# Pooled attention and mixture of depths on one core: leftover products of two token chunks together, other chunks, counts that read PSUM, another order

## The chip, the cores and the metric

One core of a Trainium2 chip runs the whole program. The metric is the device time of one execution in microseconds (us), lower is better. The engines: TensorE (PE in the profile, its weight loads PEld), VectorE (DVE), ScalarE (ACT), GpSimd (POOL), SyncE (SP, which here only issues DMAs).

## The reference, cut to what matters

```python
# q, k, v: (8 batches, 8 heads, 576 tokens, 64) float32
k_p = k.reshape(B, H, 72, 8, D).mean(axis=3)          # 8 tokens pooled to 1: 72 keys
v_p = v.reshape(B, H, 72, 8, D).mean(axis=3)
attn = softmax(q @ k_p.T / sqrt(D))
x = heads side by side of (attn @ v_p)                 # (8, 576, 512)
scores = einsum('bsd,d->bs', x, w_gate); out = x.copy()
for b in range(B):
    top = the 128 tokens of the largest scores[b]
    ye = relu(x[b, top] @ w1) @ w2                     # w1 512x1024, w2 1024x512
    out[b, top] = x[b, top] + sigmoid(scores[b, top])[:, None] * ye
```

Everything is float32. A batch is 3.5 MB of q, k and v; w1 and w2 are 4 MB.

## The kernel before

Each batch passes two parts. The **front** (one per batch, 0 to 7) is attention, the store of x and the choice of 128 tokens. The **dense** part (also one per batch) is the two matrix products on those tokens and the scatter of their rows.

*Front.* SP issues the loads of k, q and v. There is one k buffer (`kr`) and there are two each of q and v, so the load of k of the next batch waits until k is pooled. k and v of batch 0 are pooled on PE, the others on DVE or POOL (L530, L531; L618 to L624). DVE transposes pooled k (L539) and q (L558, in two halves of 16 and 20 of the 36 steps). The scores are made with the keys on the partitions. 72 keys don't fit two heads on 128 partitions, so the last 64 keys of each head are products of 32x64 tiles (L576), and the 8 *leftover keys* of four heads together are products of 128x32 tiles (L585). ACT takes the exponentials (L590 into `em`, L594 into `el`). The 576 tokens are then taken in five *chunks* (four of 128 tokens, number 4 of 64). For each chunk PE multiplies with the pooled v: 16 main products in 64x64 tiles (L663), then 4 leftover products in 64x64 tiles (L667), into one pair of PSUM banks. The columns beside v give the softmax sum and the token's score; ACT or DVE takes them (L681 to L685), DVE inverts (L689), ACT or DVE normalises into `xs` (L698, L700), and SP or ACT stores `xs` to `out` (L396).

*Rank.* When all chunks of a batch have their sums, DVE makes the scores (L716, L717), PE spreads them over all partitions (L737, a transpose of a broadcast), ACT or DVE copies that row from PSUM into `sr` (L408, L410), and for each chunk one DVE instruction counts how many scores are larger (L749, five per batch). From the ranks come a one-hot matrix (L756 to L760), on PE the list of the chosen tokens (L766), the indices (`tk`, L770; `ix`, L774 on POOL), and POOL issues an indirect DMA (L775) that gathers the 128 rows from `out` into `xr`, for which all five stores of the batch must have landed.

*Dense.* PE transposes `xr` (L796), multiplies with w1 (L805, 64 products of 128 columns per batch), ACT or DVE applies relu, PE multiplies with w2 (L819, 8 products of 512 columns), DVE makes `y` (L824), POOL scatters (L828).

*Fillers.* Eight steps named `busy` (L847) multiply the identity by itself, four products each, while PE would have nothing to do.

*Order.* A class `Plan` collects some 777 steps with engines, priorities and dependencies. What is built is fixed by three tables of numbers in the source: `ORDER` (the order of all steps), `HOMES` (the PSUM banks of each PSUM job) and `TURNS` (which of its possible engines a step takes). Each engine runs its steps in the order of the table; waits follow from the data. PSUM has 8 banks: the scores of a half take banks 0 to 3, a chunk takes one pair of four, a `ONES` job one bank.

Of the kernel before, what the change touches and what calls it, by code (L numbers as in the profile page):

```python
# [96 lines left out]
"""  # L97
TABLE = [[int(x) for x in t.split()] for t in (ORDER, HOMES, TURNS)]
ON_PE = (0,)
AGO = 500  # L100


class Plan:


    SWITCH = 0.2

    def __init__(self):
# [1147 lines left out]
```

## Time and profile before

| | |
|---|---|
| runs (us) | 249.0, 250.75, 251.26; median 250.75 |
| the profiled execution | 249.6 us; its profile spans 247.8 us |
| PE busy | 220.0 us, 89% |
| DVE, POOL, ACT busy | 146.1, 106.9, 83.4 us |
| moved by DMA | 46.82 MB |
| mean granted TensorE clock | 0.965 |

Times in the profile count from the start of the span. A busy PE is modelled from the matmuls' sizes, so how long a group of products really takes is read from the starts of the groups behind it. One float32 matmul of the program shows as two records (x32 is 16 products).

### The profile page before, as it was taken

The numbers are of one execution on the slowest core, as the hardware profiler recorded it, in microseconds if no ns is written. First come the engines' busy times: TensorE is split into PE (matmuls) and PEld (weight loads), VectorE is DVE, ScalarE is ACT, GpSimd is POOL, SyncE is SP. The second block draws the span as 40 slices with busy tenths as digits, with TensorE's granted clock in tenths as the row PEclk, the third lists the DMA queues.
The fourth block names the chain that finished last, engine by engine and source line by source line (L and its number), as shares of the span: only waits on it lengthen the run. The fifth ranks groups of instructions, "written<-read, shape, count | busy, mean of one in ns | idle before, by whom it ended". The sixth has DMA issues, their size and how long they took to land.

```text
span 247.8 us, 7329 instructions
## 1 busy us (share of the span) xinstructions
PE 220.0 (89%) x3074; PEld 155.9 (63%) x3074; DVE 146.1 (59%) x357; ACT 83.4 (34%) x282; POOL 106.9 (43%) x147
## 2 busy tenths in 40 slices
PE   2799869497959999999989999999999999999980
PEld 2497537255648935795438789674588869656740
DVE  2589985997991683896587699448094603200210
ACT  2004564675635352257236644335011000201000
POOL 7023782992695639797760534020071302210310
PEclk9999999779968999999999999999999999999996
DMA  6998999997799959839750122414312101110101
GB/s 195 363 329 307 379 354 323 393 355 277 266 314 380 335 225 346 329 128 352 296 187 4 50 103 87 127 49 129 125 46 83 28 20 42 42 42 3 52 33 56
DMA packets 16329, 46.82 MB, mean 189 GB/s; under 512 B 1696, under 2 KB 1696, under 8 KB 14496
## 3 DMA queue, kind: packets, MB, share of 16 engines
q1 hardware_dynamic: 12016, 37.23, 41.7%
q10 hardware_dynamic: 2992, 4.85, 6.1%
q0 software_dynamic: 1280, 4.20, 5.0%
q8 instruction: 26, 0.43, 0.7%
q14 instruction: 15, 0.12, 0.1%
HBM read 34.73 MB, written 11.53 MB: 187 GB/s over the span
## 4 chain that ended last, share of the span: by engine, by line
PE 60%; DMA 16%; POOL 11%; issue 5%; DVE 4%; SPq 1%; POOLq 0%; DVEq 0%; ACT 0%
PE pJ L819 10%; PE pG L805 9%; DMA xr<-out_dram,ix 8%; DMA vr<-in_v_dram 8%; PE pA L805 7%; PE pJ L805 7%; PE pG L819 6%; PE pG L663 3%; PE pA L819 3%; POOL vr L618 3%; PE pG L667 2%; PE pG L576 2%; POOL vr L623 2%; POOL vs L624 1%; POOL vr L628 1%
## 5 line engine op out<-in xcount | busy, mean ns | idle before, releaser
L819 PE MATMUL pJ<-w,ht 128*128 128x512 f32 x80 | 37.7, 602 | 0.0
L749 DVE SCALAR_TENSOR_TENSOR cmp<-sr,sc,lat 128x576 bf16<-128x576 f32 (+1 forms) x40 | 35.3, 883 | 0.9
L774 POOL TENSOR_SCALAR ix<-tk 128x1 int32<-128x1 f32 x8 | 2.9, 368 | 54.2 <-DVE gv L783 19.3
L558 DVE STREAM_TRANSPOSE qt<-qr 128x1280 f32<-128x1280 f32 (+1 forms) x16 | 21.7, 1362 | 5.7 <-DMA qr<-in_q_dram 5.7
L618 POOL TENSOR_TENSOR vr<-vr 128x512 f32<-128x512 f32 (+1 forms) x12 | 18.6, 1563 | 11.8 <-DMA vr<-in_v_dram 11.8
L805 PEld LDWEIGHTS pG<-xg,w 128*128 128x128 f32 x192 | 22.4, 192 | 1.8 <-issue 1.8
L805 PE MATMUL pG<-xg,w 128*128 128x128 f32 x192 | 23.1, 276 | 0.0
L819 PEld LDWEIGHTS pJ<-w,ht 128*128 128x128 f32 x80 | 14.0, 190 | 14.0 <-issue 13.6
L828 POOL DMA_INDIRECT out_dram<-y,ix x8 | 8.9, 1109 | 30.4 <-DVE y L824 15.0
L590 ACT ACTIVATE em<-pG 128x1280 f32<-128x1280 f32 (+1 forms) x16 | 18.1, 1129 | 11.5 <-PE pG L585 11.1
L576 PE MATMUL pG<-qt,kt 32*64 32x320 f32 (+1 forms) x512 | 20.8, 429 | 1.3 <-ACT em L590 1.3
L805 PEld LDWEIGHTS pJ<-xg,w 128*128 128x128 f32 x160 | 18.6, 192 | 1.8 <-issue 1.4
L805 PEld LDWEIGHTS pA<-xg,w 128*128 128x128 f32 x160 | 18.5, 192 | 1.8 <-issue 1.8
L805 PE MATMUL pJ<-xg,w 128*128 128x128 f32 x160 | 19.4, 277 | 0.0
L805 PE MATMUL pA<-xg,w 128*128 128x128 f32 x160 | 19.0, 276 | 0.0
L576 PEld LDWEIGHTS pG<-qt,kt 32*64 32x64 f32 x512 | 10.1, 136 | 9.1 <-issue 2.8
L819 PE MATMUL pG<-w,ht 128*128 128x512 f32 x32 | 14.4, 592 | 0.0
L824 DVE SCALAR_TENSOR_TENSOR y<-pG,gv,xr 128x512 f32<-128x512 f32 x2 | 1.5, 752 | 21.3 <-PE pG L819 21.3
L689 DVE RECIPROCAL rz<-za 128x8 f32<-128x8 f32 (+1 forms) x40 | 7.2, 189 | 11.1 <-ACT za L681 8.7
L663 PEld LDWEIGHTS pG<-vs,em 64*64 64x64 f32 x448 | 11.6, 146 | 3.5 <-issue 2.0
L698 ACT ACTIVATE xs<-pG,rz 128x64 f32<-128x64 f32 (+1 forms) x56 | 12.1, 348 | 4.0 <-DMA out_dram<-xs 3.4
L663 PEld LDWEIGHTS pA<-vs,em 64*64 64x64 f32 x416 | 9.8, 140 | 5.0 <-ACT ss L682 1.9
(171 smaller groups left out, 406.5 us busy)
## 6 DMA issues: line engine op xcount, KB each, us to landing
vr<-in_v_dram SPq DMA_DIRECT2D x8, 1024.0 KB
kr<-in_k_dram SPq DMA_DIRECT2D x7, 1152.0 KB
qr<-in_q_dram SPq DMA_DIRECT2D x7, 1152.0 KB
out_dram<-xs ACTq DMA_DIRECT2D x17, 256.0 KB
w<-in_moe_w_dram SPq DMA_DIRECT2D x4, 1024.0 KB
out_dram<-xs SPq DMA_DIRECT2D x15, 256.0 KB
vr<-in_v_dram SPq DMA_DIRECT2D x16, 64.0 KB
out_dram<-xs SPq DMA_DIRECT2D x6, 128.0 KB
```

The costliest lines, as they stand in the source:

```text
L558: nc.vector.transpose(out=QT[b % 2][h].rearrange("p j t c -> p t j c"), in_=QR[b % 2][:, lo:hi].rearrange("p t (j e) -> p t j e", j=2))
L576: note(nc.tensor.matmul(pG[64 * s : 64 * s + 64, r, 0:n], KT[i][rows, j, (SP - NL) * s + NL : (SP - NL) * s + SP], tokens(j, s, rows, 0, h ...
L590: note(nc.scalar.activation(EM[h][i], pG[:, :, 0:n], AF.Exp, scale=exp_scale))
L618: engine(e).tensor_tensor(out=x[:, a:z, 0:4], in0=x[:, a:z, 0:4], in1=x[:, a:z, 4:8], op=OP.add)
L623: engine(e).tensor_tensor(out=x[:, :, 0:2], in0=x[:, :, 0:2], in1=x[:, :, 2:4], op=OP.add)
L663: note(nc.tensor.matmul(acc[64 * z : 64 * z + 64, s, E * m : E * m + E], EM[h][i][64 * s : 64 * s + 64, m, m0 + 64 * z : m0 + 64 * z + 64] ...
L689: nc.vector.reciprocal(RZ[i][rows, c], ZA[rows, b, c])
L698: note(nc.scalar.activation(to[:, s, m], o[:, s, m, 0:D], AF.Copy, scale=rz[:, NP * s + m : NP * s + m + 1]))
L749: nc.vector.scalar_tensor_tensor(cmp[0:n], SR[0:n], SC[i][0:n, c : c + 1], LAT[0:n, LAST - OFF[c] : LAST - OFF[c] + S], op0=OP.subtract, o ...
L805: note(nc.tensor.matmul(single(ju)[:, cap * f : cap * f + cap], w1[g][:, d, 128 * f : 128 * f + 128], XG[i][:, d, :], start=(d == 0), stop ...
L819: note(nc.tensor.matmul(single(jd)[0:cap, :], HT[i][f // 4][:, f % 4, :], w2[f // 4][:, f % 4, :], start=(f == 0), stop=(f == FB - 1)))
L828: j = nc.gpsimd.indirect_dma_start(out=out_rows, out_offset=bass.IndirectOffsetOnAxis(ap=IX[x][:, :1], axis=0), in_=Y[i], in_offset=None)
```

## The change

1. **Chunks.** A chunk was 8 of the 36 steps by all 16 groups of tokens; chunks 0 to 3 are now 16 steps by 8 groups, chunk 4 is 4 steps by 16 groups. In a store, the outermost dimension is now 16 (before 8, for chunk 4 it was 4). `q` is transposed into a layout with runs of 8, and the exponentials of the second half and of the leftover keys take three ACT instructions each (`spread`) so that each chunk is contiguous in `em` and `el`.
2. **Leftover keys.** Their scores for all tokens of a batch are one step of 8 products of 320 columns in a PSUM bank of its own (before 8 of 128 and 8 of 192 columns beside the main scores). The leftover products with v now run in 32x64 tiles for two chunks together: chunks 0 with 2, 1 with 3, and 4 alone; both chunks' PSUM pairs are held until then.
3. **Rank.** The copies into `sr` are gone: the spread row stands in a pair of banks and the five counts of DVE read it there. The two sums of `tk` and `gv` are one reduction.
4. **Loads.** The gate vector is loaded in rows of 1792 bytes in place of 256.
5. **Order.** All three tables are new: 753 steps.

The diff, cut to its core (the tables left out but for one line):

```diff
-    2 4 10 21 3 12 14 31 9 19 16 8 6 13 91 18 17 22 5 36 20 15 23 11 7 37 24 25 26 38 39 40 41 770 32 33 42 34 35
+    2 4 9 19 3 5 12 10 21 11 741 16 6 14 20 0 746 17 34 29 13 18 85 22 23 24 25 8 89 26 88 87 30 7 31 35 36 15 37 38
...
-    TN = (8, 8, 8, 8, 4)
+    TN = (16, 16, 16, 16, 4)
+    GN = (8, 8, 8, 8, 16)
+    ALONG = ((0, 2), (1, 3), (4,))
...
-            nc.vector.transpose(out=QT[b % 2][h].rearrange("p j t c -> p t j c"),
-                                in_=QR[b % 2][:, lo:hi].rearrange("p t (j e) -> p t j e", j=2))
+            nc.vector.transpose(out=QT[b % 2].rearrange("p j x t g -> p t (j x) g")[:, lo:hi],
+                                in_=QR[b % 2][:, lo:hi].rearrange("p t (x g) -> p t x g", g=8))
...
-            for s in range(2):
-                for z in range(halves):
-                    note(nc.tensor.matmul(acc[64 * z : 64 * z + 64, s, 0 : NP * E], EL[h][i][64 * s : 64 * s + 64, l0 + 64 * z : l0 + 64 * z + 64],
-                                     VL[i][64 * s : 64 * s + 64, u].rearrange("p m e -> p (m e)"),
-                                     start=False, stop=True, skip_group_check=True))
+                for s in range(2):
+                    for z in range(2):
+                        for c in cs:
+                            if z < ROWS[c] // 64:
+                                x = 64 * s + 32 * SIDE[c]
+                                note(nc.tensor.matmul(pair(jobs[c])[64 * z : 64 * z + 64, s, 0 : NP * E], EL[i][x : x + 32, AT[c] + 64 * z : AT[c] + 64 * z + 64],
+                                                      VL[i][x : x + 32].rearrange("p m e -> p (m e)"),
+                                                      start=False, stop=True, skip_group_check=True), jobs[c])
...
-                copy(e, SR[:, OFF[a] : OFF[a] + w], single(j_)[:, 0:w])
...
-                nc.vector.scalar_tensor_tensor(cmp[0:n], SR[0:n], SC[i][0:n, c : c + 1], LAT[0:n, LAST - OFF[c] : LAST - OFF[c] + S],
-                                               op0=OP.subtract, op1=OP.is_gt, accum_out=RK[0:n, b, c])
+                note(nc.vector.scalar_tensor_tensor(cmp[0:n], row()[0:n, 0:S], SC[i][0:n, c : c + 1], LAT[0:n, LAST - OFF[c] : LAST - OFF[c] + S],
+                                                    op0=OP.subtract, op1=OP.is_gt, accum_out=RK[0:n, b, c]))
```

DVE, from the scores of batch 0 (`sc0`) to its token list (`tk0`), before, from the first count on (L749 counts, L689 and L700 end chunks, L558 transposes q of batch 3, L716 and L717 already make the scores of batch 1):

```order
L749 SCALAR_TENSOR_TENSOR cmp_119,rk_115<-sr_114,sc0_109,lat_116 128x576
L558 STREAM_TRANSPOSE qt11_81<-qr1_69 128x20x2x32
L749 SCALAR_TENSOR_TENSOR cmp_119,rk_115<-sr_114,sc0_109,lat_116 128x576
L689 RECIPROCAL rz1_108<-za_148 128x8
L749 SCALAR_TENSOR_TENSOR cmp_119,rk_115<-sr_114,sc0_109,lat_116 128x576
L632 TENSOR_REDUCE vs0_90<-vr0_70 128x5
L642 COPY vs0_90<-vs0_90 32x66 x2
L646 TENSOR_TENSOR vl0_92<-vs0_90,inside_160 128x528
L749 SCALAR_TENSOR_TENSOR cmp_119,rk_115<-sr_114,sc0_109,lat_116 128x576
L689 RECIPROCAL rz1_108<-za_148 128x8
L700 TENSOR_TENSOR xs10_100<-pA_169,rz1_108 128x2x4x64
L749 SCALAR_TENSOR_TENSOR cmp_119,rk_115<-sr_114,sc0_109,lat_116 64x576
```

and now (L777 makes `sc0`, L589 transposes q of batch 2, L570 pooled k of batch 2):

```order
L777 TENSOR_REDUCE sc0_105<-ss0_101 128x5
L589 STREAM_TRANSPOSE qt0_78<-qr0_68 128x20x8x8
L805 SCALAR_TENSOR_TENSOR cmp_114,rk_110<-pA_162,sc0_105,lat_111 128x576 x3
L570 STREAM_TRANSPOSE kh_73<-ks_72 128x9x64
L805 SCALAR_TENSOR_TENSOR cmp_114,rk_110<-pA_162,sc0_105,lat_111 128x576
L805 SCALAR_TENSOR_TENSOR cmp_114,rk_110<-pA_162,sc0_105,lat_111 64x576
L746 RECIPROCAL rz1_104<-za_143 128x8 x2
```

Between `sc0` and the first count there stood eleven other instructions before, now one. From the last count to `tk0` follow, now: the ends of four chunks of batch 1, `qt0` of batch 2 (first half), `kh` and `qt1` (first half) of batch 3.

PE, before the first transposed gather, of batch 0 (`xr0`), before (L576 and L585 are the scores of batch 3, L663 and L667 chunks of batch 2):

```order
L585 MATMUL pG_168<-qt11_81,kl1_77 32x192 x8
L663 MATMUL pA_169<-vs0_90,em10_84 64x66 x8
L667 MATMUL pA_169<-vl0_92,el10_88 64x264 x2
L663 MATMUL pJ_170<-vs0_90,em00_82 64x66 x16
L667 MATMUL pJ_170<-vl0_92,el00_86 64x264 x4
L576 MATMUL pG_168<-qt10_80,kt1_75 64x256 x16
L585 MATMUL pG_168<-qt10_80,kl1_77 32x128 x8
L796 MATMUL pA_169<-ident_151,xr0_132 128x128 x4
L663 MATMUL pJ_170<-vs1_91,em11_85 64x66 x16
```

and now (L611 and L628 are the scores of batch 3, L798 spreads the scores of batch 1, L702 and L714 are chunks of batch 2):

```order
L611 MATMUL pG_161<-qt1_79,kt1_75 64x256 x16
L798 MATMUL pJ_163<-ident_146,sc1_106 128x128 x4
L798 MATMUL pJ_163<-ident_146,sc1_106 128x64
L611 MATMUL pG_161<-qt1_79,kt1_75 64x320 x16
L628 MATMUL pA_162<-qt1_79,kl1_77 32x320 x8
L849 MATMUL pA_162<-ident_146,xr0_127 128x128 x4
L702 MATMUL pG_161<-vs0_86,em00_80 64x66 x16
L702 MATMUL pG_161<-vs0_86,em10_82 64x66 x16
L714 MATMUL pG_161<-vl0_88,el0_84 64x264 x8
L702 MATMUL pJ_163<-vs0_86,em10_82 64x66 x8
L714 MATMUL pJ_163<-vl0_88,el0_84 64x264 x2
```

The transposed gather (L796, now L849) stood behind all five chunks of batch 2 and stands now ahead of them; all eight fillers now stand ahead of it, before seven (the eighth was at the end). On POOL the first gather stood behind the pooled v of batches 2 and 3, and stands now behind that of batch 2 alone. On SP, the first half of w1 came after k, q and v of batches 0 to 3, and comes now after k and q of batch 4 as well.

## Rows read from the trace of the kernel before

**Rows 1.** The page, part 1: busy time, share of span and instructions.

```profile
PE 220.0 (89%) x3074; PEld 155.9 (63%) x3074; DVE 146.1 (59%) x357; ACT 83.4 (34%) x282; POOL 106.9 (43%) x147
```

**Rows 2.** Windows: stretch and length in us, busy us by engine, clock, DMA share, GB/s.

```profile
0.00:60.00 60.00, 45.11 (x869) 31.52 (x869) 45.75 (x84) 24.73 (x92) 33.33 (x57) 0.94 0.92 327
0.00:70.97 70.97, 53.14 (x1044) 36.97 (x1044) 55.21 (x105) 31.59 (x111) 39.92 (x64) 0.94 0.91 323
46.00:53.00 7.00, 6.29 (x128) 3.84 (x128) 6.91 (x14) 5.37 (x24) 6.76 (x7) 0.51 1.04 379
70.00:77.00 7.00, 6.03 (x124) 4.62 (x124) 4.48 (x12) 0.58 (x1) 4.28 (x6) 0.52 1.02 353
70.97:239.70 168.73, 165.90 (x2023) 118.20 (x2024) 89.83 (x249) 51.81 (x171) 65.96 (x83) 0.98 0.40 140
```

**Rows 3.** Timeline of PE, 0 to 75 us: start, length, what, idle before.

```profile
46.71 1.16 PE L663 MATMUL pJ<-vs,em 64*64 64x66 f32 x32 [3.68 <-ACT xs L698]
...
70.97 1.09 PE L796 MATMUL pA<-ident,xr 128*128 128x128 f32 x4 [2.94 <-DMA xr<-out_dram,ix]
```

**Rows 4.** Timeline of DVE, 10 to 75 us: the rank of batch 0.

```profile
33.48 0.20 DVE L717 TENSOR_REDUCE sc<-ss 128x5 f32<-128x40 f32 x1 [0.26 <-DVE ss L716]
...
63.67 0.12 DVE L770 TENSOR_REDUCE tk<-pA 128x1 f32<-128x2 f32 x1
```

**Rows 5.** The chain of waits in order of time: start, length, what.

```profile
63.88 0.82 POOL ix L774
...
64.99 5.84 DMA xr<-out_dram,ix
...
85.84 7.53 DMA xr<-out_dram,ix
...
130.09 1.05 PE pG L576 x32
131.14 0.57 PE pG L585 x16
...
154.81 1.26 PE pG L576 x32
156.07 0.79 PE pG L585 x16
...
239.71 0.76 DVE y L824
```

**Rows 6.** Timeline of PE in two chunks, 138 to 140 us.

```profile
138.41 0.70 PE L663 MATMUL pJ<-vs,em 64*64 64x66 f32 x32
138.93 0.62 PE L667 MATMUL pJ<-vl,el 64*64 64x264 f32 x8
139.37 0.65 PE L663 MATMUL pG<-vs,em 64*64 64x66 f32 x32
139.84 0.72 PE L667 MATMUL pG<-vl,el 64*64 64x264 f32 x8
```

**Rows 7.** Groups by line and shape: busy us, mean ns of one, idle before.

```profile
L749 DVE SCALAR_TENSOR_TENSOR cmp<-sr,sc,lat 128x576 bf16<-128x576 f32 x32 | 28.9, 902 | 0.6
L558 DVE STREAM_TRANSPOSE qt<-qr 128x1280 f32<-128x1280 f32 x8 | 12.0, 1501 | 5.7 <-DMA qr<-in_q_dram 5.7
L558 DVE STREAM_TRANSPOSE qt<-qr 128x1024 f32<-128x1024 f32 x8 | 9.8, 1222 | 0.0
L539 DVE STREAM_TRANSPOSE kh<-ks 128x576 f32<-128x576 f32 x8 | 9.7, 1214 | 0.1
L689 DVE RECIPROCAL rz<-za 128x8 f32<-128x8 f32 x32 | 6.0, 192 | 5.9 <-ACT za L681 4.6 <-ACT ht L812 1.2
L749 DVE DVE_READ_ACCUMULATOR cmp<-sr,sc,lat 128x1 f32 x32 | 2.6, 81 | 0.0
L700 DVE TENSOR_TENSOR xs<-pA,rz 128x512 f32<-128x512 f32 x7 | 4.8, 692 | 0.4
L847 PE MATMUL pG<-ident 128*128 128x128 f32 x40 | 5.4, 283 | 0.0
```

More of the change, by code (lines that the diff above doesn't have):

```diff
@@ L147, in listed @@
         for o in ops:
-            if o["job"] is not None:
-                jobleft[o["job"]] += 1
+            for j in (o["job"], o["job2"]):
+                if j is not None:
+                    jobleft[j] += 1
         ready = [0.0] * len(ops)
@@ L159, in listed @@
         order = []
+        mates = {}
+        for o in ops:
+            if o["job2"] is not None:
+                mates[o["job"]], mates[o["job2"]] = o["job2"], o["job"]
+        first = {}
+        for n, o in enumerate(ops):
+            if o["job"] is not None:
+                first.setdefault(o["job"], n)
+        due = []
         def homes(j):
@@ L163, in homes @@
                 return None
+            if due and j not in due:
+                return 1e9, None
+            if j in mates and not due:
+                if left[first[mates[j]]] or sum(all(held[x] is None for x in h) for h in self.jobs[j]) < 2:
+                    return 1e9, None
             best = None
@@ L213, in listed @@
             order.append(n)
-            j = o["job"]
-            if j is not None:
+            for j in (o["job"], o["job2"]):
+                if j is None:
+                    continue
                 jobend[j] = max(jobend[j], done)
@@ L368, in direct_path, with note @@
     beside = {}
-    def note(ins):
+    def note(ins, other=None):
         n, e, j, needs = plan.now
+        if other is not None:
+            j = other
         if j is None:
@@ L642, in again @@
                     nc.vector.tensor_copy(to, of)
-        both((("DVE", 0.35), ("ACT", 0.42)), False, again, [("VS", i)], [("VS2", i)], p, name=f"vd{b}")
+        both((("DVE", 0.42), ("ACT", 0.5)), False, again, [("VS", i)], [("VS2", i)], p, name=f"vd{b}")
         def spread(e):
             engine(e).tensor_tensor(
-                out=VL[i].rearrange("p u m e -> p (u m) e"),
-                in0=VS[i][:, NP : NP + 1, :].to_broadcast([128, 2 * NP, E]),
-                in1=inside.rearrange("p u (m one) -> p (u m) one", one=1).to_broadcast([128, 2 * NP, E]), op=OP.mult)
@@ new lines, in spread, with attend, main, go @@
+                out=VL[i], in0=VS[i][:, NP : NP + 1, :].to_broadcast([128, NP, E]),
+                in1=inside.rearrange("p (m one) -> p m one", one=1).to_broadcast([128, NP, E]), op=OP.mult)
+        both((("DVE", 0.4), ("POOL", 0.62)), False, spread, [("VS", i), ("VS2", i), "VS1", "inside"], [("VL", i)], p, name=f"vl{b}")
+    def attend(b):
+        i = b % 2
+        jobs = [plan.job(PAIRS) for c in range(NC)]
+        def main(c):
+            h, j_ = int(SIDE[c]), jobs[c]
+            def go():
+                acc = pair(j_)
+                for m in range(NP):
+                    for s in range(2):
+                        for z in range(ROWS[c] // 64):
+                            note(nc.tensor.matmul(acc[64 * z : 64 * z + 64, s, E * m : E * m + E],
+                                                  EM[h][i][64 * s : 64 * s + 64, m, AT[c] + 64 * z : AT[c] + 64 * z + 64],
+                                                  VS[i][64 * s : 64 * s + 64, m, :], start=(m == 0), stop=False, skip_group_check=True))
+            add("PE", 0.52, go, [("EM", h, i), ("VS", i), ("VS2", i), "VS1"], [], 100 * b + 5 + c, mode=6464, job=j_, name=f"a{b}{c}")
+        def more(cs):
+            def go():
+                for s in range(2):
+                    for z in range(2):
[5 more added lines that the diff above has]
+                                                      start=False, stop=True, skip_group_check=True), jobs[c])
+            add("PE", 0.5, go, [("EL", i), ("VL", i)], [], 100 * b + 5 + cs[-1], mode=3264, job=jobs[cs[0]],
+                job2=jobs[cs[1]] if len(cs) > 1 else None, name=f"al{b}{cs[0]}")
+        for cs in ALONG:
+            for c in cs:
+                main(c)
+            more(cs)
+        for c in range(NC):
+            after(b, c, jobs[c])
@@ L672, in attend, with after @@
+    def after(b, c, j_):
+        n, i = ROWS[c], b % 2
         rows = slice(0, n)
@@ L707, in kept @@
             store.setdefault(b, []).append(x)
-        dma(out[b].rearrange("(g t) d -> t g d", g=G)[T0[c] : T0[c] + TN[c]], XS[i][c][rows], n * 2048, 100 * b + 4,
-            [("XS", i, c)], [("ROWS", b, c)], then=kept, rate=260e3, cost=0.62, free=True, name=f"o{b}{c}")
+        to = out[b].rearrange("(g t) d -> t g d", g=G)[T0[c] : T0[c] + TN[c], G0[c] : G0[c] + GN[c]]
+        if c == NC - 1:
+            to = to.rearrange("t g d -> g t d")
+        dma(to, XS[i][c][rows], n * 2048, 100 * b + 4,
+            [("XS", i, c)], [("ROWS", b, c)], then=kept, rate=360e3, cost=0.68, free=True, name=f"o{b}{c}")
     def rank(b):
@@ L717, in score @@
             nc.vector.tensor_reduce(out=SC[i], in_=SS[i], axis=AX.X, op=OP.add)
-        add("DVE", 0.76, score, [("RZ", i, c) for c in range(NC)], [("SC", i)] + [("SS", i, c) for c in range(NC)], p - 70,
+        add("DVE", 0.52, score, [("RZ", i, c) for c in range(NC)], [("SC", i)] + [("SS", i, c) for c in range(NC)], p - 70,
             name=f"sc{b}")
@@ L722, in pieces, with row, spread @@
             a, g = AUX[i], engine(e)
-            g.tensor_copy(a[:, :, 2], SC[i])
-            g.tensor_tensor(out=R1, in0=SC[i], in1=a[:, :, 2], op=OP.subtract)
-            g.tensor_copy(a[:, :, 3], R1)
-            g.tensor_tensor(out=R1, in0=R1, in1=a[:, :, 3], op=OP.subtract)
+            g.tensor_copy(a[:, :, 3], SC[i])
+            g.tensor_tensor(out=R1, in0=SC[i], in1=a[:, :, 3], op=OP.subtract)
             g.tensor_copy(a[:, :, 4], R1)
+            g.tensor_tensor(out=R1, in0=R1, in1=a[:, :, 4], op=OP.subtract)
+            g.tensor_copy(a[:, :, 5], R1)
         both((("DVE", 0.9), ("POOL", 1.45)), False, pieces, [("SC", i), "AUX0"], [("AUX", i), "R1"], p - 65, name=f"pc{b}")
-        for half, (a, z) in enumerate(((0, 3), (3, NC))):
-            w = sum(ROWS[a:z])
-            j_ = plan.job(ONES)
-            def spread(a=a, z=z, j_=j_):
-                for c in range(a, z):
-                    o = OFF[c] - OFF[a]
-                    note(nc.tensor.transpose(single(j_)[:, o : o + 128], SC[i][:, c : c + 1].to_broadcast([128, 128]), ident))
-            add("PE", 0.115 * (z - a) + 0.05, spread, [("SC", i), "ident"], [], p - 70, job=j_, name=f"sp{b}{half}")
-            def keep(e, a=a, w=w, j_=j_):
-                copy(e, SR[:, OFF[a] : OFF[a] + w], single(j_)[:, 0:w])
-            both((("DVE", 0.12 + 1.05e-3 * w), ("ACT", 0.15 + 0.87e-3 * w)), False, keep, [], [("SR", half)], p - 70, job=j_,
-                 name=f"ke{b}{half}")
+        jr = plan.job(PAIRS)
+        def row():
+            return pair(jr).rearrange("p a b -> p (a b)")
+        def spread():
+            for c in range(NC):
+                n = ROWS[c]
+                note(nc.tensor.transpose(row()[:, OFF[c] : OFF[c] + n], SC[i][0:n, c : c + 1].to_broadcast([n, 128]), ident[0:n, 0:n]))
+        add("PE", 0.72, spread, [("SC", i), "ident"], [], p - 70, job=jr, name=f"sp{b}")
         for c in range(NC):
@@ L760, in one_hot @@
                     nc.vector.tensor_scalar(OH[:, c, :], slots, RK[:, b, c], None, op0=OP.is_equal)
-        both((("DVE", 1.45), ("ACT", 2.1)), True, one_hot, [("RK", b, c) for c in range(NC)] + ["slots", "ones"], ["OH"], p + 0.6, name=f"oh{b}")
+        both((("DVE", 1.35), ("ACT", 2.45)), True, one_hot, [("RK", b, c) for c in range(NC)] + ["slots", "ones"], ["OH"], p + 0.6, name=f"oh{b}")
         j_ = plan.job(ONES)
```

179 lines of the change are left out of this document (90 added, 89 removed), and 85 rows, old and new, of tables (HOMES, ORDER, TURNS).

## The prediction

> **What bounds the kernel now.** I read the page first: PE is busy 220.0 of 247.8 us, DVE 146.1 [rows 1], so the kernel ends when PE has done its work, and only two things matter: how much work that is, and where PE stands idle or runs at a lower clock. The windows cut the span at 70.97 us, where PE transposes the first gathered rows and dense work begins [rows 2, 3]. Behind that point PE is busy 165.90 of 168.73 us, 2.8 us idle. Ahead of it PE is busy 53.14 of 70.97, 17.8 us idle, while DMA moves 327 GB/s over the first 60 us. In two stretches of 7 us, at 46 and at 70 us, the granted clock is 0.51 and 0.52, half of it at 1.2 GHz in place of 2.4 [rows 2]; PE had idled 3.68 and 2.94 us just before [rows 3]. At half speed the 6.29 and 6.03 busy us are 3.1 and 3.0 us of work, so the second part of each is lost.
>
> In full-speed time PE does 53.14 - 3.1 = 50.0 us of work ahead of 70.97 and 165.90 - 3.0 = 162.9 behind it, 212.9 together. From the end of its last product (239.71) to the end of the span are 8.1 us, and 1.8 us more to the execution's own 249.6.
>
> Why 70.97? The chain of waits and the timeline of DVE tell: the scores of batch 0 exist at 33.68 [rows 4], but its token list only at 63.67. Then the path is fixed: index, indirect DMA, PE starts 7.3 us after the list's start [rows 3 to 5]. Thirty us of rank for five counts of 0.90 + 0.08 us [rows 7] is order and not work: other instructions of DVE stand between.
>
> **The change, part by part.**
>
> *First gather (order, counts from PSUM).* This is the largest term. In the new order one transpose stands between the scores and the counts, and behind them four chunk ends, two transposes of q and two of k before the list. I sum DVE from the durations [rows 7]: one q transpose 1.50; five counts of 0.98, 4.9; two k transposes 2.4; four inversions and normalisations of 0.19 + 0.69, 3.5; one pair of small copies from PSUM, which I set at 0.3; two q transposes 2.4. That is 15.1 us. Ahead of the scores the same attention of batch 0 must be done, so I keep 33.68: the list at 48.8. The other path to it is data: the transpose of q of batch 3 stands right before the list. Up to that q SP and ACT issue (sizes from the tensors' shapes) four batches of k and q, 9.4 MB, v 4.7, gate 0.2, five stores 1.2: 15.5 MB, at 327 GB/s [rows 2] 47.4 us, plus 1.22 for the transpose 48.6. Both paths agree. With 7.3 us the first transposed gather starts at 56.2; the second gather of the trace took 7.53 against 5.84 [rows 5], which would be 57.9. I take **57**, 14 us earlier. What is late next: the first half of w1, now behind k and q of batch 4. Up to it 19.5 MB, 59.6 us; PE has batch 2's five chunks to do there (4.3 us), so it hides.
>
> *Work done by then.* Of the 50.0 us, five chunks of batch 2 are no longer ahead: a chunk is 0.47 + 0.44 [rows 6], 4.6 us. One more filler is, 1.1 (40 records, 8 to a filler, are 5.4 us [rows 7]).
>
> *Scores of leftover keys.* Products of 192 columns took 0.79, of 128 0.57 [rows 5], so 64 columns are 0.22 and the fixed part is 0.13. One step of 320 in place of two saves 0.13, over 8 batches 1.1 us. The main scores keep columns and shape.
>
> *Leftover products.* Within the 64x64 tiles a chunk's leftover takes 0.44 [rows 6]. Two chunks together on 32-row tiles take the same 264 columns once, if their eight products run beside each other as those of L576 do: 64 columns there cost 0.21, the time of two rounds of 64, for 16 products [rows 5]. Five times 0.44 becomes three times: -0.88 per batch. Against it stands the change of tile shape, three times in and out. Rows 5 give a fixed part of 1.05 - 4 x 0.21 = 0.21 for L576 and 0.57 - 2 x 0.22 = 0.13 for L585; a chunk's main products right behind another shape take 0.52 against 0.47 [rows 6]. I take 0.15 in and 0.05 out, three times 0.20: net -0.3, over 8 batches **-2.4 us**. The bounds: no cost at all, -7.0; 0.21 both ways, +3.0. The Trainium skill speaks against this part: "TensorEngine Tiling (Array Packing)", Key Properties, says that changing the tiling mode drains TensorE. The fixed parts of rows 5 agree with it; without the rule the sum would end 4.6 us lower.
>
> *Transposes of q.* Their output now lies in runs of 8 elements. The trace has runs of 32 (1.17 ns per element) and, for k, single elements nine apart (2.1 ns) [rows 7]. Runs of 8 are nearer the first; I take no cost. The other end is 0.9 ns x 2304 = 2.1 us of DVE per batch.
>
> *Three exponentials for one, twice per batch:* ACT is busy 34% [rows 1] and has room for some 0.5 us per batch; without that cover it delays the banks of the scores by as much. *Copies into `sr` gone, fewer reductions:* some 1 us per batch less for DVE and ACT, inside the idle time of both once PE is the bound. *Stores, gate:* they change how the same bytes move; hidden behind PE after 57 us, and before it only 1.2 MB are stores. *PSUM:* the spread row now holds a pair of banks until the last count; zero if PE has other steps with free banks, see the rivals.
>
> **The sum.** Work ahead of the gather: 50.0 - 4.6 + 1.1 - 0.5 (four score steps) - 0.6 (two batches' chunks) = 45.4. Work in all: 212.9 + 1.1 - 1.1 - 2.4 = 210.5. Behind the gather: 165.1. From 57 that is 222.1; idle time behind it as before 2.8 plus 1 for the tighter first steps; one stretch at half clock half the time, as PE will still idle some us ahead of 57: 1.5. End of PE 227.4, plus 8.1 and 1.8: 237.3 against the profiled 249.6, which lies 1.15 under the median of the runs. So **238** us on the scale of the runs.
>
> **Rivals.**
>
> 1. *Only half of the early gain* (0.20). DVE doesn't run through its queue: it is busy 55.21 of the first 70.97 us [rows 2] and every instruction ahead of the list can wait for POOL or PE. Dear transposes alone (seven halves ahead of the list, 7 us) would do it. Gather at 64: 245.
> 2. *The gather is early and nothing follows* (0.12). The windows show DMA at 327 GB/s from the start; if w1 or k of batch 4 lands 10 us after my 59.6, since k has one buffer and POOL must empty it, PE waits there what it waited before. Left is the work saved, some 2 to 3 us: 248.
> 3. *The other side: PSUM held by the counts* (0.09). Before, a copy freed the bank after about half a us; now two of eight banks stay taken for at least 4.9 us of counts, longer where transposes stand between, and in the order the chunk that takes the pair next (of batch 1) stands directly behind. If PE waits for it in each of the 8 ranks, the gain of 12.7 is gone at 1.6 us per rank; at 2 us it is 254. For it: DVE is the second busiest engine and no longer lets a copy by ACT pass ahead. Against it: behind 70.97 PE found work nearly always (2.8 us idle), the step moved is one of many, and DVE is busy only 89.83 of 168.73 us there.
>
> The forecast itself has 0.59.
>
> **How the numbers follow.** The predicted time is the forecast's, 238. Its own range is 233 (no cost of the tile shape) to 243. The stated range adds rivals 1 and 2: 232 to 249. A measurement of this kernel tells about 1% from no change, 248.2 to 253.3. Faster by more: the forecast and rival 1, 0.79; within 1%: rival 2, 0.12; slower: rival 3, 0.09.
>
> **What would show it.** The first L849 on PE at 55 to 59 us, `tk` of batch 0 at about 49. PE's busy time some 2 to 9 us lower, with at most one stretch of half clock ahead of 60 us. Starts of two chunks' leftover products (L714) 0.55 to 0.65 us before the next step; if 0.9 or more, they don't run beside each other. L589 at 1.2 and 1.5 us. The count (L805) at 0.8 to 0.9. Idle time of PE behind the gather 3 to 5 us; much of it ended by L805 is rival 3, by a load of w1 rival 2. I would be wrong if the first gather stays behind 65 us, or if PE, having it early, idles later by as much.

## The result and the profile after

| | before | after |
|---|---|---|
| runs (us) | 249.0, 249.47, 250.75, 251.26; median 250.11 | 240.16, 241.38, 241.96, 242.09; median 241.67 |
| profiled execution, its span | 249.6, 247.8 | 240.16, 238.3 |

The ratio is 0.965, 95% interval 0.959 to 0.972: faster, where 238 was forecast in a range of 232 to 249. The page's first part, against [rows 1]:

```profile
PE 212.4 (89%) x2946; PEld 146.9 (62%) x2946; DVE 137.0 (58%) x347; ACT 76.1 (32%) x253; POOL 102.9 (43%) x170
```

The windows of the new kernel, cut at its first transposed gather, and one short stretch behind it (columns as in [rows 2]):

```profile
0.00:60.00 60.00, 46.22 (x862) 31.99 (x865) 43.02 (x95) 24.29 (x78) 38.33 (x74) 1.00 0.96 356
0.00:58.65 58.65, 44.87 (x808) 30.81 (x808) 43.02 (x95) 23.71 (x77) 37.05 (x72) 1.00 0.96 355
58.65:229.10 170.45, 167.46 (x2139) 116.11 (x2139) 93.07 (x248) 52.40 (x176) 64.90 (x98) 0.99 0.44 151
60.00:65.00 5.00, 5.00 (x136) 3.26 (x136) 2.29 (x9) 0.00 (x0) 2.36 (x3) 0.66 0.52 195
```

Ahead of the gather the granted clock is no longer halved (0.50, 1.2 GHz in place of 2.4); behind it there is one such stretch, of 3.4 us, in the last row, and PE idles 3.0 us in all. The timelines of DVE, POOL and PE, from the scores of batch 0 to the two gathers that PE waited for (against [rows 3, 4]):

```profile
32.30 0.20 DVE L777 TENSOR_REDUCE sc<-ss 128x5 f32<-128x40 f32 x1
...
49.18 0.16 DVE L826 TENSOR_REDUCE tk<-pJ 128x2 f32<-128x6 f32 x1 [2.00 <-PE pJ L822]
...
50.47 1.20 POOL L831 DMA_INDIRECT xr<-out_dram,ix  x1 [0.79 <-DMA kr<-in_k_dram]
...
58.65 0.66 PE L849 MATMUL pA<-ident,xr 128*128 128x128 f32 x4 [3.50 <-DMA xr<-out_dram,ix]
...
109.65 0.63 PE L849 MATMUL pG<-ident,xr 128*128 128x128 f32 x4 [2.99 <-DMA xr<-out_dram,ix]
```

In the chain of waits that gather takes longer than the 5.84 of [rows 5]:

```profile
50.47 8.13 DMA xr<-out_dram,ix
```

**A budget of PE.** From the start of PE's first product to the start of its last one I add the time from each product's start to the next one's; what of it no product covers is idle time, and of a stretch at half clock half is counted as lost. (Idle time so found agrees with the windows: before 17.83 + 2.83 less the 4.61 us to the first product, 16.05.)

| us | work at full clock | fillers | idle | lost to half clock | sum |
|---|---|---|---|---|---|
| before | 205.7 | 8.1 | 16.1 | 6.0 | 235.9 |
| after | 202.0 | 8.5 | 11.2 | 1.7 | 223.4 |

Of 12.5 us, 3.7 are less work, 4.9 less idle time, 4.3 less half clock; 0.4 more of fillers goes against them. The span gains 9.5: the first product starts 1.0 later (5.61 against 4.61), and 2.0 lie behind the last one. The order of the loads (the larger of k's two now comes first) explains at most about half of the 1.0: in the twelve runs below, with the same order of these loads, the first product starts at 4.88 to 5.16.

The work is not known to a tenth. In the eleven runs below that leave PE's products as they are, or take out fillers alone, it comes to 202.3 to 204.6; the profile here has the least, 202.0. So the 3.7 could be as little as 1.1.

### The profile page after: what moved, and what is told of

Read it like the earlier page. It is cut to its first block, busy times and chain, and to the rows that moved or that the text cites. A ratio compares the mean times of both kernels' runs of the same rounds, so it can differ in the third digit from the quotient of the medians.

```text
span 238.3 us, 7049 instructions
## 1 busy us (share of the span) xinstructions
PE 212.4 (89%) x2946; PEld 146.9 (62%) x2946; DVE 137.0 (58%) x347; ACT 76.1 (32%) x253; POOL 102.9 (43%) x170
## 4 chain that ended last, share of the span: by engine, by line
PE 68%; DMA 13%; POOL 9%; issue 4%; DVE 1%; SPq 1%; POOLq 0%; ACT 0%; DVEq 0%
PE pJ L858 16%; PE pJ L872 15%; PE pG L872 9%; DMA xr<-out_dram,ix 7%; DMA vr<-in_v_dram 6%; PE pG L858 5%; PE pG L611 4%; PE pG L702 4%; PE pG L714 3%; POOL kr L561 2%; PE pA L702 2%; PE pA L858 2%; PE pJ L628 1%; POOL ks L562 1%; SPq L421 1%
## 5 line engine op out<-in xcount | busy, mean ns | idle before, releaser
L858 PEld LDWEIGHTS pJ<-xg,w 128*128 128x128 f32 x352 | 41.4, 192 | 5.4 <-issue 4.4
L858 PE MATMUL pJ<-xg,w 128*128 128x128 f32 x352 | 44.1, 278 | 0.0
L595 ACT ACTIVATE em<-pG 128x1024 f32<-128x1024 f32 x16 | 16.4, 1028 | 39.7 <-PE pG L611 39.7
L872 PE MATMUL pG<-w,ht 128*128 128x512 f32 x48 | 22.3, 594 | 0.0
L805 DVE SCALAR_TENSOR_TENSOR cmp<-pA,sc,lat 128x576 bf16<-128x576 f32 (+1 forms) x25 | 20.1, 804 | 3.7 <-PE pA L798 3.1
L611 PE MATMUL pG<-qt,kt 32*64 32x320 f32 (+1 forms) x512 | 20.6, 413 | 1.4 <-issue 1.0
L589 DVE STREAM_TRANSPOSE qt<-qr 128x1280 f32<-128x1280 f32 (+1 forms) x16 | 21.8, 1367 | 0.0
L611 PEld LDWEIGHTS pG<-qt,kt 32*64 32x64 f32 x512 | 10.1, 131 | 10.5 <-issue 5.9
L561 POOL TENSOR_TENSOR kr<-kr 128x512 f32<-128x512 f32 (+1 forms) x9 | 13.8, 1531 | 6.2 <-DMA kr<-in_k_dram 6.2
L662 POOL TENSOR_TENSOR vr<-vr 128x640 f32<-128x640 f32 x7 | 10.8, 1540 | 9.1 <-issue 8.9
L755 ACT ACTIVATE xs<-pG,rz 128x64 f32<-128x64 f32 (+1 forms) x56 | 12.1, 339 | 6.6 <-PE pG L714 3.8
L702 PE MATMUL pG<-vs,em 64*64 64x66 f32 x640 | 13.7, 223 | 0.0
L872 PEld LDWEIGHTS pG<-w,ht 128*128 128x128 f32 x48 | 8.6, 190 | 8.1 <-issue 8.1
L702 PEld LDWEIGHTS pG<-vs,em 64*64 64x64 f32 x640 | 11.9, 135 | 2.5 <-issue 1.0
L805 DVE SCALAR_TENSOR_TENSOR cmp<-pG,sc,lat 128x576 bf16<-128x576 f32 (+1 forms) x10 | 8.1, 810 | 8.0 <-PE pG L798 7.8
```

What stands on the lines that cost most here:

```text
L561: e.tensor_tensor(out=x[:, a:z, 0:2], in0=x[:, a:z, 0:2], in1=x[:, a:z, 2:4], op=OP.add)
L589: nc.vector.transpose(out=QT[b % 2].rearrange("p j x t g -> p t (j x) g")[:, lo:hi], in_=QR[b % 2][:, lo:hi].rearrange("p t (x g) -> p t x ...
L595: note(nc.scalar.activation(to[:, :, 0:256].rearrange("p m (h x) -> p m h x", h=2), of[:, :, :, 0:16].rearrange("p m h t g -> p m h (t g)" ...
L611: note(nc.tensor.matmul(pG[64 * s : 64 * s + 64, r, 0:n], KT[i][rows, j, (SP - NL) * s + NL : (SP - NL) * s + SP], QT[i][rows, j, 2 * s : ...
L662: engine(e).tensor_tensor(out=x[:, :, 0:2], in0=x[:, :, 0:2], in1=x[:, :, 2:4], op=OP.add)
L702: note(nc.tensor.matmul(acc[64 * z : 64 * z + 64, s, E * m : E * m + E], EM[h][i][64 * s : 64 * s + 64, m, AT[c] + 64 * z : AT[c] + 64 * z ...
```

## The experiments

All have the changed kernel as their base. The ratio is to the kernel before on the same chip; the changed kernel's own is 0.965, interval 0.959 to 0.972. Where two intervals overlap, the kernels are not told apart. The last four columns are the budget of one profiled run each, in us.

| kernel | median us | ratio, 95% interval | work | fillers | idle | half clock |
|---|---|---|---|---|---|---|
| late_gather | 245.1 | 0.976, 0.967 to 0.985 | 203.7 | 8.5 | 10.9 | 7.7 |
| no_two_fillers | 243.5 | 0.974, 0.964 to 0.984 | 204.4 | 6.2 | 13.9 | 1.7 |
| loads_behind | 242.7 | 0.966, 0.956 to 0.977 | 203.7 | 8.5 | 12.1 | 3.4 |
| stores_8 | 254.4 | 1.012, 0.999 to 1.024 | 204.0 | 8.5 | 18.1 | 8.0 |
| stores_cols | 250.2 | 0.997, 0.991 to 1.004 | 203.7 | 8.7 | 15.7 | 5.1 |
| exp_split | 241.7 | 0.979, 0.968 to 0.989 | 202.3 | 8.6 | 11.9 | 3.4 |
| stores_gt | 246.6 | 0.994, 0.989 to 0.999 | 203.4 | 8.6 | 13.0 | 6.1 |
| leftover_64 | 247.7 | 0.987, 0.981 to 0.993 | 207.7 | 8.5 | 10.2 | 3.4 |
| counts_copy | 249.6 | 0.996, 0.989 to 1.004 | 203.0 | 8.5 | 16.2 | 5.1 |
| ix2_early | 241.0 | 0.961, 0.956 to 0.967 | 203.4 | 8.6 | 10.6 | 3.4 |
| tu2_behind | 240.3 | 0.967, 0.958 to 0.976 | 204.6 | 8.6 | 9.4 | 3.2 |
| best | 238.7 | 0.962, 0.956 to 0.968 | 204.2 | 8.4 | 8.9 | 3.4 |

Where only the order changed, the diffs below show the steps of an engine by their names, a letter or more and the batch, with the part or chunk behind it: `ix0` is index and gather of batch 0, `tu0` the transposes of its rows, `a20` the main products of chunk 0 of batch 2, `al` leftover products, `s`, `sl` scores, `sp` spread, `pk` list, `u` products with w1, `k`, `q`, `v` loads, `w10` and `w20` the first halves of w1 and w2, `o` stores, `va`, `vb`, `vg`, `vl`, `kt`, `kl` steps of pooling. In late_gather, tu2_behind and best one or two PSUM jobs also have other banks.

**late_gather**

```diff
 POOL  ... vb2 kt3
-ix0
 vg2 kl3 va30 va31 vl2 vb3 vg3
+ix0
 PE    ... s31 sl3
-tu0
 a20 a22 al20 a24 al24 a23 a21 al21
+tu0
```

> The changed kernel with one thing put back: the index and the gather of batch 0 stand on POOL behind the pooling of v of batch 3 (some 7 us later), and PE transposes them behind the chunks of batch 2, which are then done while the gather is under way. All work is the same. Theory (the end follows the start of the dense part, since PE finds work almost all the time behind it): the first transpose of gathered rows at 64 to 66 in place of 58.65, with 2.7 us of chunks moved ahead of it, so the end 3 to 5 us later: 244 to 247. Rival (the gain lies in the cheaper parts, and the order of the first gather is hidden): 241 to 242.5, as the changed kernel's 241.7.

First transposes at 64.89, time 245.1: the place and the size that the theory gave. But its reason holds only in part: idle time is 10.9 against 11.2, and the difference is half clock, 7.7 against 1.7, in three stretches (at 44, 64 and 112 us; the first also comes and goes between profiles of unchanged code, see the last section). The profile is that of the longest of four runs, but all four say the same: their mean granted clocks are 0.952 to 0.970, those of the changed kernel 0.974 to 0.984. By the ratio the loss is 1.1%, and the intervals overlap.

**no_two_fillers**

```diff
-            for x in range(4):
+            for x in range(0 if i in (1, 7) else 4):
```

> The changed kernel without the products of the two fillers (busy1, busy7) that stand on PE between the chunks of batch 1 and the list of batch 0. Theory (the list waited 2.0 us for PE, which stood behind these fillers): list of batch 0 at 47 to 47.5 in place of 49.18, the gather some 1 to 2 us earlier unless it lands behind the same loads, end at 239.5 to 241. Rival (the fillers keep the clock up, and without them PE runs at half clock for some us ahead of the gather): no gain or 1 to 3 us lost, 241.5 to 244, with a stretch of clock near 0.5 ahead of 58 us.

The list came at 47.84, after a wait of 0.40 in place of 2.00, and PE started on the gather at 57.46, without half clock ahead of it. The time did not fall. Of the 2.3 us of fillers left out 2.7 came back as idle time. The first link of the theory is shown, its end fell. The rival's half clock is not in the profile, but that is the shortest of the four runs, with a mean clock of 0.979; the two longest (244.7 and 244.9) have 0.964 and 0.958, and no profile shows where they lost it.

**loads_behind**

```diff
 SP    k4
-q4
 w10
-w20
 v40
+q4
 w11 o13
+w20
```

> The changed kernel with two loads moved back in the SP queue: q of batch 4 and the first half of w2 are issued behind the loads that wait until 53 us, so that between 44 and 53 us only k of batch 4 and the first half of w1 are issued. Theory A (the first gather took 8.13 us because 4.5 MB of loads lay in the DMA queues ahead of it): the gather takes 4 to 6 us, first transpose of gathered rows at 55 to 57, end 239 to 241. Theory B (the gather's own 128 rows and the stores it waits for take that long): 8 us as now, 241 to 242.5. Against both: q of batch 4 comes 4 us later, and if the scores of batch 4 wait for it, what is gained ahead is lost behind.

The list came at 49.81. The gather was issued at 52.89, when the last store of batch 0 had landed, and PE, which did not wait for it, began on it at 56.57: at most 3.7 us in place of 8.1, theory A. That it was issued 2.4 us later is not the reason: in ix2_early, with the loads where they were, the first gather was issued at 52.53 and took 7.0. What was won is given back: behind the gather PE is busy 170.70 of 176.13 us, 5.4 idle against 3.0, and the ratio is the changed kernel's.

**stores_8** and **stores_cols**. Each store in two issues, by rows (outermost dimension 8) or by columns (outermost dimension 16):

```diff
-            i = engine(e).dma_start(out=dst, in_=src)
+            for y in range(2 if then else 1):
+                m = src.shape[0] // 2
+                i = engine(e).dma_start(out=dst[8 * y : 8 * y + 8], in_=src[m * y : m * y + m]) if then else engine(e).dma_start(out=dst, in_=src)
...
+                i = engine(e).dma_start(out=dst[:, :, 256 * y : 256 * y + 256], in_=src[:, 256 * y : 256 * y + 256]) if then else engine(e).dma_start(out=dst, in_=src)
```

(`then` is set for stores alone.)

> The changed kernel with each store of x issued as two of half the rows, outermost dimension 8 in place of 16, so that each spreads over 8 DMA engines; one issue of some 0.7 us more per store is the price on SP and ACT. Theory (the stores hide behind PE; the DMA rate of 356 GB/s in the first 60 us comes from loads issued earlier and from the order): 355 to 330 GB/s in the first 60 us, first gather 0 to 2 us later, end 241.5 to 244. Rival (stores over 16 engines make the rate, and so the early gather): 325 to 335 GB/s, first gather 3 to 6 us later, end 245 to 249.

> The changed kernel with each store of x issued as two, of the left and the right 256 columns: as many issues as in stores_8, but the outermost dimension stays 16. Theory (stores_8 lost 12 us since its stores ran over 8 of 16 DMA engines and landed late: the gather of batch 0 stood on POOL from 51.8 to 59.9): here the gather is issued at 50 to 53 and the end stays at 241.5 to 245. Rival (the second issue of each store, some 0.7 us on SP or ACT, holds up the loads and the exponentials behind it): gather at 56 to 60, end at 249 to 255.

Both lost the whole gain, so my theory of either run fell; stores_8 went past its rival too, and the rival of stores_cols held (gather issued at 57.82, time 250.2). **exp_split** and **stores_gt** separate the two causes with one issue per store:

```diff
-        note(nc.scalar.activation(to[:, :, 0:256].rearrange("p m (h x) -> p m h x", h=2),
-                                  of[:, :, :, 0:16].rearrange("p m h t g -> p m h (t g)"), AF.Exp, scale=exp_scale))
+        for h in range(2):
+            note(nc.scalar.activation(to[:, :, 128 * h : 128 * h + 128].rearrange("p m (t g) -> p m t g", g=8),
+                                      of[:, :, h, 0:16], AF.Exp, scale=exp_scale))
...
-        if c == NC - 1:
-            to = to.rearrange("t g d -> g t d")
+        to = to.rearrange("t g d -> g t d")
```

(The first part is exp_split; stores_gt has "(g t)" in it, the second part, and token numbers to match. exp_split stayed at 241.7, as its theory had it; its ratio, 0.979, is higher than the changed kernel's, with intervals that overlap.)

> The changed kernel with the first exponential of each step in two instructions, one per half of the groups: the same elements, one fixed cost more on ACT for each (three per batch). It is the control for stores_gt, which needs this split. Theory (ACT, busy for a third of the span, hides some 0.2 us three times per batch): 241 to 243.5. Rival (the banks of the scores come free later, and in this tight order every delay of ACT reaches PE): 244 to 247.

> As exp_split, but with the rows of chunks 0 to 3 in the order of groups and then steps: the exponentials are written with a stride, the token numbers follow, and each store has outermost dimension 8 in place of 16 with one issue as before. It separates what stores_8 and stores_cols left mixed. Theory A (with stores on 8 of 16 DMA engines they land late behind the loads, and the first gather waits for them): gather issued at 54 to 58 in place of 50.5, end 4 to 10 us above exp_split. Theory B (stores_8 and stores_cols lost by their second issue on ACT and SP alone): end within 2 us of exp_split.

The gather of batch 0 waits for its index and the batch's five stores. The lines of `tk` and of the gather, DVE and POOL, in exp_split:

```profile
49.32 0.16 DVE L828 TENSOR_REDUCE tk<-pJ 128x2 f32<-128x6 f32 x1 [1.62 <-PE pJ L824]
50.62 1.20 POOL L833 DMA_INDIRECT xr<-out_dram,ix  x1 [0.79 <-DMA kr<-in_k_dram]
```

in stores_gt:

```profile
52.28 0.16 DVE L827 TENSOR_REDUCE tk<-pJ 128x2 f32<-128x6 f32 x1 [2.98 <-PE pJ L823]
55.90 1.20 POOL L832 DMA_INDIRECT xr<-out_dram,ix  x1 [3.12 <-DMA out_dram<-xs]
```

in stores_cols:

```profile
51.72 0.16 DVE L827 TENSOR_REDUCE tk<-pJ 128x2 f32<-128x6 f32 x1 [2.70 <-PE pJ L823]
57.82 1.20 POOL L832 DMA_INDIRECT xr<-out_dram,ix  x1 [5.60 <-DMA w<-in_moe_w_dram]
```

and in stores_8:

```profile
51.34 0.16 DVE L828 TENSOR_REDUCE tk<-pJ 128x2 f32<-128x6 f32 x1 [2.15 <-PE pJ L824]
59.91 1.21 POOL L833 DMA_INDIRECT xr<-out_dram,ix  x1 [8.08 <-DMA w<-in_moe_w_dram]
```

From the list to the gather's issue it takes 1.3, 3.6, 6.1 and 8.6 us. (The `w` named there is what landed last; the program waits for the stores.) These times don't price the stores by themselves, since the lists came at different times and a gather that waits for a store doesn't wait for its list. The last store of batch 0, of chunk 2, which ACT issues, tells more. In us; it has landed with the last update of its semaphore in the trace:

| kernel | outermost, issues | last issue | landed | under way | gather issued |
|---|---|---|---|---|---|
| exp_split | 16, one | 41.46 | 48.79 | 7.3 | 50.62 |
| stores_gt | 8, one | 43.17 | 54.94 | 11.8 | 55.90 |
| stores_cols | 16, two | 47.78 | 56.72 | 8.9 | 57.82 |
| stores_8 | 8, two | 47.72 | 58.81 | 11.1 | 59.91 |

In exp_split it landed before the list; in the other three the gather followed it by 1.0 to 1.1 us. With an outermost dimension of 8 the store was under way 4.4 and 2.2 us longer, theory A of stores_gt. With two issues the last one left 6.3 and 4.6 us later, since ACT waited for an earlier store first; in stores_cols:

```profile
45.27 0.27 ACT L739 ACTIVATE za<-pJ,eps 128x8 f32<-128x8 f32 x1 [3.94 <-DMA out_dram<-xs]
```

The gather came 5.3 us later by the one, 7.2 by the other and 9.3 by both, so the two don't simply add up. Meanwhile POOL stands, and the pooling queued behind it comes late. Not all of stores_gt's loss need be this: its exponentials, written with a stride, took 1066 ns in place of 598, 12.4 us more of ACT's busy time, and no run separates the two. Its list was 3.0 us later, but so it was in runs with unchanged code there (see the last section).

The Trainium skill, "DMA: Bandwidth & Descriptors", section "Why a DMA increments its semaphore by 16 and not by 1", says that a transfer is spread over the largest number of engines up to 16 that divides the slowest dimension of both sides. The trace agrees: this store raises its semaphore 16 times as it lands in exp_split, and once at its issue and eight times as it lands in stores_gt. That the fewer engines make it slower is likely and not shown.

**leftover_64**

```diff
-                                x = 64 * s + 32 * SIDE[c]
+                                x = 64 * s
...
-                                                      VL[i][x : x + 32].rearrange("p m e -> p (m e)"),
+                                                      VL[i][x : x + 64, int(SIDE[c])].rearrange("p m e -> p (m e)"),
```

> The changed kernel with the leftover products back on 64x64 tiles, the tile shape of the main products: each chunk takes its 4 products of 64 rows, of which the pooled values of the other half's keys are zero, so two chunks no longer run beside each other and no tile shape changes between main and leftover products. DVE or POOL writes pooled values twice as wide (some 0.4 us more per batch). Theory (after the switch of shape the grouping saves next to nothing: 1.73 and 1.20 us per pair and single chunk against 0.91 per chunk): PE busy within 2 us of now, end 240.5 to 243. Rival 1 (grouping saves the forecast 0.3 us per batch, 2.4 in all): 244 to 245. Rival 2 (it costs more than it saves): 237 to 240.

The theory fell, and rival 1 was too small. Main and leftover products together take, by the budget, 40.7 us before, 35.2 after and 40.4 here. The loss of some 5.5 us in the time is this work, 5.2 us more of it: idle time is lower than after (10.2).

**counts_copy**

```diff
+                if c == 0:
+                    copy("DVE", SR, row()[:, 0:S])
-                note(nc.vector.scalar_tensor_tensor(cmp[0:n], row()[0:n, 0:S], SC[i][0:n, c : c + 1], ...
+                nc.vector.scalar_tensor_tensor(cmp[0:n], SR[0:n], SC[i][0:n, c : c + 1], ...
```

> The changed kernel with the copy of the spread row back: DVE copies it from PSUM ahead of the first count, and the five counts read the copy, so the pair of banks is free after the copy. Theory (what the counts read decides little: DVE gets some 0.75 us more per batch, the first list comes 0.7 to 1.5 us later, and POOL runs slower beside counts): 242 to 244.5. Rival 1 (reading PSUM is the larger part of the gain): 246 or more. Rival 2 (the banks held by the counts cost PE time, so the copy gains): 238 to 240.5.

Rival 1. The first part of its page:

```profile
PE 216.8 (88%) x2946; PEld 150.1 (61%) x2946; DVE 156.0 (63%) x355; ACT 76.7 (31%) x253; POOL 113.7 (46%) x170
```

its counts, by line (ns: minimum, median, maximum):

```profile
L809 DVE SCALAR_TENSOR_TENSOR cmp<-sr,sc,lat x40: 728/819/2762, 34.8 to 198.1; 128x576 bf16<-128x576 f32 x32, 64x576 bf16<-64x576 f32 x8
```

and the same line of the changed kernel, here the 25 of its 40 counts that read one pair of banks:

```profile
L805 DVE SCALAR_TENSOR_TENSOR cmp<-pA,sc,lat x25: 745/812/819, 34.0 to 187.9; 128x576 bf16<-128x576 f32 x20, 64x576 bf16<-64x576 f32 x5
```

The medians are the same; the maximum is 2762 ns against 819. DVE is busy 19.0 us more, only some 6 of it the eight copies of 0.75, and POOL 10.8 us more with the same instructions. The 16 counts of over 1 us all ran beside an instruction of POOL; where none ran, a count took 0.82 at most. The first gather came no later (58.19): what is lost, 5.0 us of idle time and 3.4 of half clock, lies behind it. The Trainium skill, "SBUF — State Buffer", section "SBUF: two separate sides", says that a DVE instruction with two inputs in SBUF and a GpSimd instruction that reads SBUF exclude each other for their whole length. The numbers here agree with it.

The loss holds for this order. In the kernel before the counts read `sr` too, and took 902 ns in the mean [rows 7], 35.3 us in all; they take 32.3 in the changed kernel and 47.3 here. There 5 of 40 counts took over 1 us, here 16.

**ix2_early**, **tu2_behind** and **best** go for the 3 us of idle time at 107 to 110:

```diff
 POOL  ... va50
-vb5 vg5
 ix2
+vb5 vg5
...
 PE    ... u103
-tu2
 a54 a51 a53 al51 al54
+tu2
...
 PE    ... al10
-busy1
 s21
-busy7
 a14 al14 s20 pk0 sl2 s30 sp1 s31 sl3
+busy1 busy7
 tu0
```

(The three parts are ix2_early, tu2_behind, and what best adds to tu2_behind.)

> The changed kernel with one step moved on POOL: the index and gather of batch 2 stand ahead of two steps of pooling v of batch 5 in place of behind them; the list exists at 98.1, the index was made at 101.63. Theory (the one idle gap of PE behind the first gather, 2.99 us at 107 to 110, ends with this gather's landing, so it closes, and with it the half clock that such a gap brings in some runs): gather issued at 98.4 to 98.8, no idle before its transposes, pooled v of batch 5 some 1.4 us later, end 237.5 to 240. Rival (the gap moves to the chunks of batch 5, which then wait for v, or the gather lands no earlier for the loads ahead of it): 241 to 242.5.

> The changed kernel with one step moved on PE: the transposes of batch 2's gathered rows stand behind the chunks 4, 1 and 3 of batch 5 in place of ahead of them (ACT's copy of them comes behind a one-hot matrix). Theory (PE idles 2.99 us for this gather at 107 to 110 while the inputs of these chunks exist at 106.2): the gap closes, idle time behind the first gather falls from 3.1 to below 1 us, end 237.5 to 240. Rival (later steps of batch 2 or the lists of later batches wait in its place): 241 to 242.5.

> As tu2_behind, and the two fillers busy1 and busy7 moved from ahead of batch 0's list on PE to directly ahead of the transposes of the first gather. Theory (the list no longer waits for them, as in no_two_fillers where it came at 47.84, and the 3 us before the gather lands are filled so that no half clock follows): list at 47.5 to 48.5, first transposes at 57 to 58.5 with under 1.5 us idle before them, no half clock at 60, end 235.5 to 239. Rival (the tighter start only moves idle time behind the gather, as in no_two_fillers and loads_behind): 239 to 242.

ix2_early left 2.1 us of that gap, and its time is the rival's. tu2_behind closed it; idle time is the second lowest, and the time, 240.3, lies just above its theory. In best the list came at 48.68, and the gap ahead of the first gather closed but for 1.13 us:

```profile
57.75 0.66 PE L848 MATMUL pA<-ident,xr 128*128 128x128 f32 x4 [1.13 <-DMA xr<-out_dram,ix]
```

Its median is the lowest and within its theory, its idle time 2.2 us below the changed kernel's, but 3.4 us went to half clock in the profiled run, the longest of six. With 0.962 against 0.965 and intervals that overlap it isn't shown faster than the changed kernel.

An early rank in the kernel before, without the other parts, was not tried.

## Why the prediction was right, and where it was not

- **Bound, list, rank: right, its time partly by luck.** The list of batch 0 came at 49.18 (forecast 48.8). DVE was through at 47.18, 1.6 us early (the scores came at 32.50, and its counts were shorter, 0.81 + 0.08 against the 0.98 I used), and then waited 2.00 us for PE, which I had not seen. That the two cancel is luck.
- **First gather: 1.65 us later than 57.** I took 7.3 us from list to PE, bounded by 7.53 for the gather alone; the gather took 8.13. loads_behind shows why: with two loads moved back at most 3.7 were enough. DMA moved 356 GB/s in the first 60 us in place of 327, which I had not forecast either: SP issued k and q of batch 4 and the first halves of w1 and w2 by 46 us, as its timeline shows:

```profile
43.94 0.33 SPq L421 DMA_DIRECT2D kr<-in_k_dram  x1
44.36 0.76 SPq L421 DMA_DIRECT2D qr<-in_q_dram  x1
45.18 1.13 SPq L421 DMA_DIRECT2D w<-in_moe_w_dram  x2
```

  Early loads and an early gather share the DMA engines, busy 0.96 of these 60 us.
- **Work ahead 45.4, in all 210.5: measured 44.87 and 210.6** (202.0 and 8.5 of fillers). The sum is right, its terms are not. *Leftover products* were set at -2.4 and measured -5.5 against before and -5.2 in leftover_64: by the budget 40 leftover groups took 19.5 us before and 24 take 13.5 now, 0.49 and 0.56 us each, so five times 0.49 became three times 0.56. The other tile shape costs 0.07 per group in this line; with the main products' line, 21.2 before, 21.7 now and 19.9 in leftover_64, it is some 0.10 to 0.13 (an estimate from these sums), not the 0.20 I took. In the timeline of PE, where a group lasts until the next step's start, 0.63 for two chunks and 0.59 for one (against [rows 6]):

```profile
24.13 0.65 PE L702 MATMUL pA<-vs,em 64*64 64x66 f32 x32
24.71 0.43 PE L714 MATMUL pA<-vl,el 32*64 32x264 f32 x1
...
25.34 0.69 PE L702 MATMUL pG<-vs,em 64*64 64x66 f32 x16
25.95 0.66 PE L714 MATMUL pG<-vl,el 32*64 32x264 f32 x4
26.54 0.71 PE L900 MATMUL pJ<-ident 128*128 128x128 f32 x4
```

  The Trainium skill, "TensorEngine Tiling (Array Packing)", section "Key Properties", names a drain of TensorE at such a change; the rows agree in direction, at about half of my price. Against the saving stand terms I had at nothing: the products with w1 took 59.6 us in place of 58.2, the main scores 19.5 for 18.7, the spread 6.0 for 4.9. *Leftover scores* were right (-1.4 for -1.1), and so were the *transposes of q*, 1367 ns in the mean of both halves, as in [rows 7]:

```profile
L589 DVE STREAM_TRANSPOSE qt<-qr 128x1280 f32<-128x1280 f32 (+1 forms) x16 | 21.8, 1367 | 0.0
```

- **Half clock: right in the profile.** One stretch was forecast at 1.5 us lost, 1.7 measured. But the profile is of the shortest of the four runs, with a mean clock of 0.984; the others have 0.974 to 0.979, which is 1 to 2 us more lost (an estimate: 0.005 to 0.010 of 240 us).
- **Idle time behind the gather: 3.0 for 3.8**, nearly all of it one gap that I did not name, the gather of batch 2. No wait of PE ends at a count (rival 3) or a load of w1 (rival 2).
- **End: 229.1 for 227.4**, and 9.2 us behind it where I took 8.1.
- **"they change how the same bytes move; hidden behind PE after 57 us" (stores) failed.** It overlooked that the gather waits for the stores. In stores_gt, with 8 in place of 16, the gather was issued 5.3 us later than in exp_split.
- **Copies into `sr` gone, "inside the idle time of both", failed.** In the new order the price is not the copy but what DVE and POOL do to each other while counts read SBUF; in the kernel before it was smaller. Rival 3 even had the wrong sign: holding two banks for five counts cost PE no wait, and a copy that frees them at once cost 8 us.

So the mechanism forecast (early rank, early dense part, little idle behind) is what the profile shows. The size came out smaller: 12.7 us were forecast, 8.4 measured, since the gather was later by 1.65 us, the end behind the last product longer by 1.1, and the median run lies 1.5 above the profiled one. That the work agreed is luck: an error of -3.1 (leftover products) and three of +3.3 together (w1, main scores, spread) cancelled.

What I can't give is a split of the gain by parts. Undoing the order of the first gather alone cost 1.1% of the time before, which is not clear of the noise, the leftover tiles 2.2%, the copies 3.1%. The sum is more than the 3.5% that was gained; the likely reason, not shown, is that the order was made for all parts together and each delay also brings idle time and half clock of its own. So for the largest term of the forecast, the early gather, the evidence is the budget of one profile before and one after; no run isolates it.

## What to carry to other kernels

When work moves forward, list everything that the first dependent transfer waits for, its stores and the loads queued ahead of it too: what landed long before it was needed, when the transfer came 14 us later, is on the path now. Price a copy from PSUM to SBUF by who else uses SBUF while it is read, not by its own length. In an order fixed by a table, undoing one part measures that part and the misfit of the order together; a budget of work, idle time and lost clock helps to tell the two apart.

## What the runs showed that was not expected

- The same code ahead of batch 0's list gave it at 49.18, 51.24 (ix2_early) and 52.36 us (tu2_behind). The two later ones had a stretch of 3.4 us at half clock at 45 us, behind an idle gap of PE of 2.5 and 2.3 us put down to "issue"; the changed kernel's gap there was 1.6. The length of the gap doesn't decide it: loads_behind had 2.7 and no such stretch, stores_gt 1.9 and one. Seven of the twelve runs have the stretch, at 44 to 46 us. The edits of both runs act behind the list, so such a difference between two profiles is no effect of an edit.
- The first gather, of 128 rows, took from at most 3.7 us (loads_behind) to 8.1 (the changed kernel), depending on the loads issued before it.
- An exponential that writes single elements 16 apart takes 1066 ns where contiguous runs take 598, for 512 elements per partition.
